# Bucket attention and a rational feed-forward on one core: a table of steps with pair 2's bits, pair 3's k and seven loads in other places

## The chip, the core and the metric

The kernel runs on 1 core of one Trainium2 chip. A core has TensorE (PE, with its weight loads PEld), VectorE (DVE), ScalarE (ACT), GpSimd (POOL) and a queue of transfers on SyncE (SP), which issues in its own order; the transfers of all queues share 16 DMA engines. The metric is device microseconds of one execution.

## What is computed

Two stages follow each other. Attention in which a query sees only keys of its own bucket (six sign bits of a projection), over 4 batches of 8 heads, 768 tokens and 64 channels; then a feed-forward whose activation is a quotient of polynomials, over 3072 tokens.

```python
q_bits = (np.einsum('bhsd,dk->bhsk', q, proj) > 0).astype(np.int64)
k_bits = (np.einsum('bhsd,dk->bhsk', k, proj) > 0).astype(np.int64)
mask = q_bucket[:, :, :, None] == k_bucket[:, :, None, :]
scores = scale * np.matmul(q, k.transpose(0, 1, 3, 2))
scores = np.where(mask, scores, -1000000000.0)
scores = scores - np.max(scores, axis=-1, keepdims=True)
attn = np.exp(scores)
attn = attn / (np.sum(attn, axis=-1, keepdims=True) + 1e-09)
return np.matmul(attn, v).astype(np.float32)
...
h = x @ w_in
P = a[0] + a[1] * h + a[2] * h2 + a[3] * h3
Q = 1.0 + np.abs(b[0]) * np.abs(h) + np.abs(b[1]) * h2
g = P / (Q + 1e-06)
return (g @ w_out).astype(np.float32)
```

w_in and w_out arrive as 64-bit floats, q, k and v as 32-bit floats.

## The kernel before

**Pairs and steps.** Two heads make a pair; there are 16 pairs (0 to 15). A pair's scores are made in 12 steps: six key tiles of 128 for the first 384 queries, then six for the second. In each step TensorE makes two products a head into `pss` (a high part with the mask rows, 77 rows, and a cross product of high and low parts, 128 rows), ScalarE takes their exponential into one of nine tiles E, and GpSimd adds E into a sum `acc`. After six steps TensorE multiplies the six E by v (`psv`, 24 products), and once a pair it adds up `acc` over the partitions (`psu`). A "stretch" of a pair, below, is the time in which its 12 steps run.

**What is prepared ahead.** While a pair's scores run, later pairs are prepared. For a pair p: `load` brings q and k (`qkf`, two transfers of 384 KB); `high` rounds them to the fast matrix format (ScalarE); `low` subtracts, which leaves the low part `lo` (one instruction for q, t=0, one for k, t=1; on VectorE for later pairs, on GpSimd for early ones); `bits` multiplies two pairs at once by the projection (`psb`) and compares on VectorE (`mb`); `penalties` scales the bits; `maskrows` moves them into the operand tiles (four small transfers); `high_move`, `second_low` and `second_high` are transfers that lay the parts out. `maxstep` makes products `psm`, whose row maxima VectorE reduces into `m`; the maxima are transposed (`shift_turn`, TensorE `pst`, VectorE `mt`) and moved in as one more row (`shift_rows`).

**Weights.** Between the steps 32 tiles of weights are turned from 64-bit floats into a high and a low part: even tiles from w_in, odd ones from w_out, 512 KB each into `wr` (two buffers). Tile i has its transfer first, then two operations on ScalarE (`ws`, `wr`), three on VectorE (`psx`), a cast on ScalarE and a subtraction on VectorE. A pair's stretch has one tile of w_in and one of w_out.

**What sets the order.** Every engine and SP's queue run in the order in which the program is written; nothing reorders. The order comes from a table: `at(p, s, f, ...)` (line 501) files a call under the number 12 p + s, and `spread` (line 504) files the steps of a generator, as those of `weights` (line 451). All calls are then made in the order of these numbers, equal ones in the order of filing. The numbers stand in the dictionaries `MID` (most pairs), `FIRST` (pairs 0 to 2), `FIRST3` (pair 3's low parts) and `LAST`. So `load=4.04` in `MID` issues pair p's load behind step 4 of pair p - 4. The buffers of `qkf` are two: pair 4's load needs pair 2's high and low parts and bits done.

**After the pairs** the feed-forward runs in 96 steps of 24 products; in pair 15's stretch its first tokens are read back from memory (`xl`, `xh`).

Of the kernel before, what the change touches and what calls it, by code (L numbers as in the profile page):

```python
# [25 lines left out]
NPAIR = B * NHP  # L26
# [15 lines left out]
MID = dict(  # L42
    group=6, values=[0.66, 0.05], values_col=[1.5, 1.5], values_out=[2.5, 2.5],
    maxima=[6.54, 7.17, 8.32, 9.1, 10.1, 11.02, 12.25, 13.03, 14.15, 15.17, 16.01, 17.02], sums=17.05, sums_store=18.9,
    high=[-0.975, -0.974], low=[-0.946, 3.3, 3.35], bits=-0.945, penalties=4.02, high_move=1.9, maskrows=4.03, second_low=-2.2,
    second_high=2.69, load_v=10.99, shift_turn=5.67, shift_rows=8.82, load=4.04, recips=[23.5, 35.02, 35.3],
    weights=[[1.44, 5.01, 5.015, 5.06, 5.07, 5.08, 5.09, 5.3], [8.05, 11.005, 11.006, 11.022, 11.023, 11.024, 11.0255, 11.0256, 19.32, 21.22]],
    late_weights=[[1.44, 5.1, 5.11, 5.5, 5.65, 5.66, 11.02, 11.023], [8.05, 11.021, 11.022, 11.022, 11.024, 11.0245, 17.05, 17.665, 19.32, 21.22]],
    defer={5: 11.0252, 10: 17.1, 11: 17.2}, weights_last=[0.5, 0.8, 1.0, 1.2],
)  # L50

FIRST = dict(
    maxima1=[-0.072, -0.05, 5.52, 5.97, 6.42, 6.87, 7.32, 7.77, 8.22, 8.67, 9.12, 9.57], maxima2=9.5, rate2=0.82, high=[3.25, 3.53],
    low=[6.0, 7.45], bits=7.4, penalties=7.45, high_move=4.53, maskrows=8.2, second_low=-24.19, second_high=4.35, load_v=4.78, group=2,
    values=[-1.07, 2.65, 2.32, 2.35, 0.35, 0.61], values_out=3.02, high1=[-3.0, -3.2], low1=[-2.8, -2.95],
    high_move1=-2.7, load2=-2.6, load3=3.8, load4=10.2, penalties1=-24.26, maskrows1=-24.2,
    weights=[[-27.25, 5.45, 5.455, 5.55, 5.56, 7.35, 17.55, 18.3], [8.03, 9.04, 9.23, 9.24, 9.25, 9.26, 9.3, 11.9, 12.5, 46.81]],
    warm0=9, warm1=1, warm=3, warms=[3, 3, 3, 0, 1, 0], maxima00=[-4.3, -2.3, -4.2, -0.9, -1.2, -0.8], shift00=[-1.0, -0.2],
    shift0=[-0.08, -0.075], ahead=3, scores=[[-0.85, -0.4, -0.1], [0.1, 0.3, 0.4]], pen01=[-2.9, -0.35],
    second_high0=[-3.42, -3.4, -3.3, -3.25], load_v0=-3.3, bits1=-0.3, comp1=[-0.28, -0.27],  # L60
    maxima0=[-24.05, -23.8, -23.5, -0.9, -0.7, -0.1], turn1=[8.46, 13.26], rows1=[8.6, 14.35], turn2=8.61, third=6.9,
    third_weights=[1.44, 5.01, 5.015, 5.06, 5.07, 5.08, 5.09, 5.3], steps={3: -1.0, 4: -0.8, 5: -0.6, 6: 5.4, 7: 6.5},
)

FIRST3 = dict(low=[0.05, 3.3, 3.35])

LAST = dict(
    group=6, values=[0.28, 0.44], values_out=0.46, vout14=[3.5, 3.03],
    hi14=17.05, weights15=[5.1, 5.11],
    tokens=[[-15.0, -11.5, -8.6, -4.9], [-7.43, -4.5, -2.83, -1.09], [1.1, 4.2, 5.45, 6.3]], terms=1.0, ffn=[13.61, 16.09, 16.14],  # L70
    sums=16.96, wide=8, share=6, third=0, sums14=14.69, weights14=1.44, sumst14=22.46,
)
TINY = 2.0 ** -80

# [35 lines left out]
def bucket_attention_then_rational_ffn(ctx, tc, qT, kT, v, proj, w_in, w_out, coef, consts, out):  # L110
# [56 lines left out]
    def operands_to_terms():  # L167
# [3 lines left out]

    tail.tile([P, 32], F32, tag="below", name="below")
    last = attention(tc, nc, raw, ps_b, tail, tokens, early, operands_to_terms, ffn, load, QF, KF, v, w_in, w_out, wo_d, ident, cst,
                     ones, prj, wi_hi, wi_lo, x_d, s_d, r_d, coefficients)
    ffn.rest(ctx, last)
# [3 lines left out]
def attention(ctx, tc, nc, raw, ps_b, tail, tokens, early, operands_to_terms, ffn, load, QF, KF, v, w_in, w_out, wo_d, ident, cst, ones, prj,  # L179
# [255 lines left out]
    def recips(bb):  # L435
        n = 2 * NHP * S // P
        s = tail.tile([P, n], F32, tag="rs", name=f"rs{bb}")
        nc.sync.dma_start(s, s_d[bb].rearrange("h (x c) -> (h x) c", c=n))
        yield
        z = bank(f"psr{bb}")[:, 0:n] if bb < B - 1 else tail.tile([P, n], F32, tag="rz", name=f"rz{bb}")  # L440
        nc.vector.tensor_scalar(out=z, in0=s, scalar1=0.0, scalar2=1e-9, op0=ALU.is_gt, op1=ALU.mult)
        nc.vector.scalar_tensor_tensor(out=z, in0=z, scalar=S * TINY, in1=s, op0=ALU.max, op1=ALU.add)
        nc.vector.reciprocal(out=s, in_=z)
        yield
        nc.sync.dma_start(r_d[bb].rearrange("h (x c) -> (h x) c", c=n), s)
        yield
# [54 lines left out]
    def at(p, s, f, *args):  # L501
        plan.setdefault(12 * p + s, []).append((f, args))

    def spread(p, steps, gen):
        for s in steps:
            at(p, s, lambda g: next(g, None), gen)

    for p in range(NPAIR):
        mid = 0 < p < NPAIR - 1
        n = MID["group"] if mid else (FIRST if p == 0 else LAST)["group"]  # L510
        for s in range(12):
            if p > 0 or s >= FIRST["ahead"]:
                at(p, FIRST["steps"].get(s, s) if p == 0 else s, scores, p, s)

            if p > 1:
                at(p - 2, FIRST["maxima2"] + FIRST["rate2"] * s if p == 2 else FIRST["third"] if p == 3 and s == 0 else MID["maxima"][s], maxstep, p, s, None, p == 2 or s not in MID["defer"])
                if p > 2 and s in MID["defer"]:
                    at(p - 2, MID["defer"][s], maxreduce, p, s)
            if s % n == n - 1:
                for i in range(s - n + 1, s + 1):  # L520
                    at(p, s + (MID["values"][s // n] if mid else (FIRST if p == 0 else LAST)["values"][s // n]), values, p, i)
            if s % NT == NT - 1 and mid and p < NPAIR - 2:
                at(p, s + MID["values_col"][s // n], values_col, p, s // NT)
            if s % NT == NT - 1:
                at(p, s + (LAST["vout14"][s // NT] if p == NPAIR - 2 else MID["values_out"][s // n] if mid else (FIRST if p == 0 else LAST)["values_out"]), values_out, p, s // NT)
        for hf in range(2):
            at(p, 6 * hf + 9, values_store, p, hf)
        if p < NPAIR - 1:
            at(p, MID["sums"] if p < NPAIR - 2 else LAST["sums14"], sums, p)
            at(p, MID["sums_store"] if p < NPAIR - 2 else LAST["sumst14"], sums_store, p)  # L530
        if p > 1:
            for t in range(2):
                at(p - 2, (MID if p > 2 else FIRST)["high"][t], high, p, t)
                at(p - 2, (MID if p > 3 else FIRST3)["low"][t + t * p % 2] if p > 2 else FIRST["low"][t], low, p, t, nc.vector if p + t > 3 else nc.gpsimd)
            if p % 2 == 0:
                at(p - 2, (MID if p > 2 else FIRST)["bits"], bits, p)
                at(p - 2, (MID if p > 2 else FIRST)["penalties"], penalties, p)
            at(p - 2, (MID if p > 2 else FIRST)["high_move"], high_move, p)
            at(p - 2, (MID if p > 2 else FIRST)["maskrows"], maskrows, p)
        if p > 0:  # L540
            at(p - 1, (MID if p > 1 else FIRST)["second_low"], second_low, p)
            at(p - 1, (MID if p > 1 else FIRST)["second_high"], second_high, p)
            at(p - 1, (MID if p > 1 else FIRST)["load_v"], load_v, p)
        if p > 1:
            at(p - 1, MID["shift_turn"] if p > 2 else FIRST["turn2"], shift_turn, p)
            at(p - 1, MID["shift_rows"], shift_rows, p)
        if p > 3:
            at(p - 4, MID["load"] if p > 4 else FIRST["load4"], load, p)
        if p % NHP == NHP - 1 and p + 1 < NPAIR:
            spread(p, MID["recips"], recips(p // NHP))  # L550
    for i in range(2 * NFC):
# [322 lines left out]
```

## Time and profile before

| | |
|---|---|
| median of 3 runs | 917.94 us (916.36 to 919.22) |
| the profiled execution's own time | 926.93 us |
| its span, first to last instruction | 925.1 us |
| mean granted TensorE clock | 0.991 |
| TensorE busy | 911.5 us (99%) |
| VectorE busy | 832.0 us (90%) |
| ScalarE busy | 652.3 us (71%) |
| GpSimd busy | 428.4 us (46%) |
| moved by DMA | 111.57 MB |

Busy time counts an engine's own instructions; register work, semaphores and the issuing of transfers are left out. A granted clock of 1.00 is TensorE at its higher level of 2.4 GHz, 0.50 at its lower one of 1.2 GHz. All recorded operations carry one source line, L99, a helper's, so the rows below tell them apart by the names of their tiles, in which buffer numbers are left out: `lo<-qkf,k` is a low part of some pair's k.

### The profile page before, as it was taken

To read this page: it belongs to the slowest core of one execution; us is meant where nothing else is said; L and a number is where in the kernel's file an instruction comes from. 1 tells how busy PE (TensorE), PEld (TensorE's weight loads), DVE (VectorE), ACT (ScalarE), POOL (GpSimd) and SP (SyncE) were. 2 spreads that over 40 slices of the span, in tenths; PEclk is the share of its full clock that TensorE was granted. 3 is DMA by queue.
4 is the path that set the end of the run, shared out by engine and by line. 5 is a ranking of instruction groups with operands and counts; after the bars stand their busy time and mean duration, and the time that the engine had idled before them with its cause. 6 is when DMAs were issued, how large, how long until landed. Compare 5 with 4: busy or idle time off the path is not lost.

```text
span 925.1 us, 13694 instructions
## 1 busy us (share of the span) xinstructions
PE 911.5 (99%) x4543; PEld 698.8 (76%) x4543; DVE 832.0 (90%) x1041; ACT 652.3 (71%) x1227; POOL 428.4 (46%) x410
## 2 busy tenths in 40 slices
PE   9979999999999999999999999999999999999998
PEld 5557776776777776678888888888888888888886
DVE  6896888888889887989998999999999999998997
ACT  7446777777777776887777667766676677667664
POOL 7666888787888888012222222222223222222221
PEclk9987999999999999999999999999999999999999
DMA  7685788878888877555402100400040003001001
GB/s 207 173 237 143 221 231 235 234 222 235 230 234 231 230 197 228 162 194 179 150 1 88 49 1 1 137 1 0 1 138 1 1 34 103 1 1 46 1 0 46
DMA packets 51243, 111.57 MB, mean 121 GB/s; under 512 B 9346, under 2 KB 20214, under 8 KB 51172
## 3 DMA queue, kind: packets, MB, share of 16 engines
q1 hardware_dynamic: 50740, 110.47, 40.4%
q8 instruction: 36, 0.59, 0.3%
q14 instruction: 35, 0.29, 0.1%
q10 hardware_dynamic: 432, 0.23, 0.1%
HBM read 56.82 MB, written 21.17 MB: 84 GB/s over the span
## 4 chain that ended last, share of the span: by engine, by line
PE 93%; DMA 3%; DVE 2%; SPq 1%; issue 0%; ACT 0%; DVEq 0%; ACTq 0%
PE psh L99 28%; PE pso L99 28%; PE pss L99 14%; PE psv L99 12%; PE psm L99 7%; DMA wr<-w_in 3%; SPq L99 1%; PE psu L99 1%; PE psb L99 1%; DVE m L99 1%; PE psw L99 1%; DVE psx L99 0%; DMA k<-k 0%; PE pst_None L99 0%; PE pst L99 0%
## 5 line engine op out<-in xcount | busy, mean ns | idle before, releaser
L99 POOL TENSOR_TENSOR gl<-c,gh 128x512 fp32r<-128x512 f32 x95 | 134.9, 1420 | 411.6 <-ACT gh L99 409.5
L99 PE MATMUL pso<-wo,gh 128*128 128x512 f32 x768 | 236.0, 389 | 0.0
L99 POOL TENSOR_TENSOR acc<-acc,E 128x384 f32<-128x384 f32 x232 | 218.6, 978 | 7.4 <-ACT E L99 7.3
L99 ACT ACTIVATE E<-pss 128x384 f32<-128x384 f32 x384 | 168.8, 494 | 73.2 <-PE pss L99 64.8
L99 DVE TENSOR_REDUCE m<-psm 128x1 f32<-128x768 f32 x192 | 180.7, 954 | 28.8 <-PE psm L99 19.5
L99 PE MATMUL pss<-q,k 128*128 128x384 f32 (+2 forms) x768 | 174.0, 350 | 0.1
L99 PEld LDWEIGHTS pso<-wo,gh 128*128 128x128 f32 x768 | 144.2, 188 | 30.0
L99 PE MATMUL psh<-xh,wi_hi 128*128 128x512 f32 x384 | 149.6, 390 | 0.0
L99 ACT ACTIVATE h<-psh 128x512 f32<-128x512 f32 x96 | 57.4, 598 | 130.7 <-PE psh L99 130.7
L99 PE MATMUL psh<-xh,wi_lo 128*128 128x512 f32 x384 | 149.4, 389 | 0.0
L99 PE MATMUL psh<-xl,wi_hi 128*128 128x512 f32 x384 | 149.4, 389 | 0.0
L99 PE MATMUL pso<-wo,gl 128*128 128x512 f32 x384 | 148.9, 389 | 0.0
L99 PEld LDWEIGHTS pss<-q,k 128*128 128x128 f32 (+2 forms) x768 | 136.7, 193 | 15.5 <-issue 8.4
L99 DVE SCALAR_TENSOR_TENSOR c<-c,ab,r 128x512 f32<-128x512 f32 x96 | 136.7, 1424 | 0.0
L99 PE MATMUL psv<-E,v 128*64 128x385 f32 x768 | 133.8, 497 | 0.0
L99 PE MATMUL psm<-k,q 76*128 76x384 f32 (+1 forms) x384 | 102.7, 350 | 6.8 <-DVE m L99 6.0
L99 PEld LDWEIGHTS psv<-E,v 128*64 128x64 f32 x768 | 52.6, 138 | 71.9 <-issue 64.4
L99 DVE SCALAR_TENSOR_TENSOR w<-h,absb,w 128x512 f32<-128x512 f32 x96 | 76.1, 793 | 15.9 <-ACT w L99 15.7
L99 POOL TENSOR_TENSOR acc<-E,E 128x384 f32<-128x384 f32 x58 | 58.4, 1026 | 57.5 <-ACT E L99 57.5
L99 PEld LDWEIGHTS psh<-xh,wi_hi 128*128 128x128 f32 x384 | 72.0, 188 | 16.1 <-ACT r L99 0.6
L99 PEld LDWEIGHTS psh<-xl,wi_hi 128*128 128x128 f32 x384 | 72.1, 188 | 15.0
L99 PEld LDWEIGHTS psh<-xh,wi_lo 128*128 128x128 f32 x384 | 72.1, 188 | 14.9
(89 smaller groups left out, 1188.9 us busy)
## 6 DMA issues: line engine op xcount, KB each, us to landing
q<-q SPq DMA_DIRECT2D x45, 192.0 KB
k<-k SPq DMA_DIRECT2D x45, 192.0 KB
wr<-w_in SPq DMA_DIRECT2D x16, 512.0 KB
wr<-w_out SPq DMA_DIRECT2D x16, 512.0 KB
wo_d<-wr SPq DMA_DIRECT2D x16, 512.0 KB
wo<-wo_d SPq DMA_DIRECT2D x16, 512.0 KB
qkf<-qT SPq DMA_DIRECT2D x16, 384.0 KB
qkf<-kT SPq DMA_DIRECT2D x16, 384.0 KB
```

What stands on the lines that cost most here:

```text
L99: return self.tc.keep_in_program_order(issue(*args, **kwargs))
```

## The change

All but two edits are numbers of the table. Even pairs' loads from pair 6 on are filed at step 11.5 of the pair four ahead, behind v (10.99), where it was 4.04; odd pairs' loads stay at 4.04. In pair 0's stretch pair 2's k low part moves from 7.45 to 6.05 and its bits from 7.4 to 7.31, which is ahead of the values of step 5 (7.32); w_out's first tile is issued at 7.34, pair 4's load at 7.35 (before: 10.2) and the second tile of w_in at 8.8 (before: 13.44). Pair 3's k low part moves from VectorE at 3.3 + 12 to GpSimd at 0.051 + 12. Late in the run a tile of w_in (number 28) and the load of the last v come sooner.

```diff
@@ MID @@
-    second_high=2.69, load_v=10.99, shift_turn=5.67, shift_rows=8.82, load=4.04, recips=[23.5, 35.02, 35.3],
+    second_high=2.69, load_v=10.99, shift_turn=5.67, shift_rows=8.82, load=[11.5, 4.04], recips=[23.5, 35.02, 35.3],
@@ FIRST @@
-    low=[6.0, 7.45], bits=7.4, penalties=7.45, high_move=4.53, maskrows=8.2, second_low=-24.19, second_high=4.35, load_v=4.78, group=2,
+    low=[6.0, 6.05], bits=7.31, penalties=7.315, high_move=4.53, maskrows=8.2, second_low=-24.19, second_high=4.35, load_v=4.78, group=2,
...
-    high_move1=-2.7, load2=-2.6, load3=3.8, load4=10.2, penalties1=-24.26, maskrows1=-24.2,
-    weights=[[-27.25, 5.45, 5.455, 5.55, 5.56, 7.35, 17.55, 18.3], [8.03, 9.04, 9.23, 9.24, 9.25, 9.26, 9.3, 11.9, 12.5, 46.81]],
+    high_move1=-2.7, load2=-2.6, load3=3.8, load4=7.35, penalties1=-24.26, maskrows1=-24.2,
+    weights=[[-27.25, 5.45, 5.455, 5.55, 5.56, 7.317, 17.55, 18.3], [7.34, 9.04, 9.23, 9.24, 9.25, 9.26, 9.3, 11.9, 12.5, 46.81]],
...
-    third_weights=[1.44, 5.01, 5.015, 5.06, 5.07, 5.08, 5.09, 5.3], steps={3: -1.0, 4: -0.8, 5: -0.6, 6: 5.4, 7: 6.5},
+    third_weights=[-3.2, 5.01, 5.015, 5.06, 5.07, 5.08, 5.09, 5.3], steps={3: -1.0, 4: -0.8, 5: -0.6, 6: 5.4, 7: 6.5},
...
-FIRST3 = dict(low=[0.05, 3.3, 3.35])
+FIRST3 = dict(low=[0.05, 3.3, 0.051])
@@ LAST @@
-    sums=16.96, wide=8, share=6, third=0, sums14=14.69, weights14=1.44, sumst14=22.46,
+    sums=16.96, wide=8, share=6, third=0, sums14=14.69, weights14=-1.0, load_v=1.5, sumst14=22.46,
@@ the calls @@
-                at(p - 2, (MID if p > 3 else FIRST3)["low"][t + t * p % 2] if p > 2 else FIRST["low"][t], low, p, t, nc.vector if p + t > 3 else nc.gpsimd)
+                at(p - 2, (MID if p > 3 else FIRST3)["low"][t + t * p % 2] if p > 2 else FIRST["low"][t], low, p, t, nc.vector if p > 3 else nc.gpsimd)
...
-            at(p - 1, (MID if p > 1 else FIRST)["load_v"], load_v, p)
+            at(p - 1, (LAST if p == NPAIR - 1 else MID if p > 1 else FIRST)["load_v"], load_v, p)
...
-            at(p - 4, MID["load"] if p > 4 else FIRST["load4"], load, p)
+            at(p - 4, MID["load"][p % 2] if p > 4 else FIRST["load4"], load, p)
```

GpSimd's queue about the start of pair 1's stretch, before (a name's first number is the pair or tile; the number at its end counts tiles and means nothing here):

```order
L99 TENSOR_TENSOR acc0_1_0_470<-acc0_1_0_470,E2_149 128x384 x2
L99 TENSOR_TENSOR lo0_3_638<-qkf3_421,q1_3_612 128x768
L99 TENSOR_TENSOR acc1_0_0_653<-E3_150,E4_151 128x384 x2
L99 TENSOR_TENSOR acc1_0_0_653<-acc1_0_0_653,E5_152 128x384 x2
L99 TENSOR_TENSOR acc1_0_0_653<-acc1_0_0_653,E6_153 128x384 x2
```

The same place now:

```order
L99 TENSOR_TENSOR acc0_1_0_472<-acc0_1_0_472,E2_149 128x384 x2
L99 TENSOR_TENSOR lo0_3_641<-qkf3_421,q1_3_615 128x768
L99 TENSOR_TENSOR lo1_3_643<-qkf3_421,k1_3_617 128x768
L99 TENSOR_TENSOR acc1_0_0_658<-E3_150,E4_151 128x384 x2
L99 TENSOR_TENSOR acc1_0_0_658<-acc1_0_0_658,E5_152 128x384 x2
L99 TENSOR_TENSOR acc1_0_0_658<-acc1_0_0_658,E6_153 128x384 x2
```

The low part of pair 3's k, lo1_3, stands behind that of its q; it has left VectorE's queue, where it stood between the maxima of steps 7 and 8 of pair 2.

SP's queue from pair 0's to pair 1's stretch, before:

```order
L99 DMA wr1_518<-w_out 128x1024
L99 DMA q1_2_417<-mb2_486 12x768
L99 DMA k1_2_419<-mb2_486 13x768
L99 DMA q1_2_417<-mb2_486 12x768
L99 DMA k1_2_419<-mb2_486 13x768
L99 DMA q1_1_246<-mt1_0_531 1x3x128 x2
L99 DMA x_d0_86<-xo0_0_516 128x384
L99 DMA q2_2_579<-lo0_2_456 64x768 x2
L99 DMA k2_2_580<-lo1_2_497 64x768 x2
L99 DMA qkf4_595<-qT 128x768
L99 DMA qkf4_595<-kT 128x768
...
L99 DMA wr2_660<-w_in 128x1024
```

The same place now:

```order
L99 DMA wr1_500<-w_out 128x1024
L99 DMA qkf4_503<-qT 128x768
L99 DMA qkf4_503<-kT 128x768
L99 DMA q1_2_417<-mb2_479 12x768
L99 DMA k1_2_419<-mb2_479 13x768
L99 DMA q1_2_417<-mb2_479 12x768
L99 DMA k1_2_419<-mb2_479 13x768
L99 DMA q1_1_246<-mt1_0_534 1x3x128 x2
L99 DMA wr2_542<-w_in 128x1024
L99 DMA x_d0_86<-xo0_0_522 128x384
L99 DMA q2_2_585<-lo0_2_456 64x768 x2
L99 DMA k2_2_586<-lo1_2_458 64x768 x2
```

Pair 4's load now stands ahead of pair 2's mask rows, and weight tile 2 ahead of pair 0's output x_d0.

SP's queue at the start of pair 3's stretch, before:

```order
L99 DMA q2_4_1136<-lo0_4_916 64x768 x2
L99 DMA k2_4_1137<-lo1_4_998 64x768 x2
L99 DMA v_3_1156<-v 128x768
L99 DMA wr6_1228<-w_in 128x1024
L99 DMA q1_5_1177<-q1_5_1177 64x768
L99 DMA k1_5_1182<-k1_5_1182 64x768
```

The same place now:

```order
L99 DMA q2_4_1133<-lo0_4_916 64x768 x2
L99 DMA k2_4_1134<-lo1_4_998 64x768 x2
L99 DMA v_3_1153<-v 128x768
L99 DMA qkf6_1196<-qT 128x768
L99 DMA qkf6_1196<-kT 128x768
L99 DMA wr6_1228<-w_in 128x1024
L99 DMA q1_5_1174<-q1_5_1174 64x768
L99 DMA k1_5_1179<-k1_5_1179 64x768
```

Pair 6's load, which stood behind pair 4's mask rows earlier in pair 2's stretch, now stands between pair 3's v and weight tile 6.

## Rows read from the trace of the kernel before

**Rows 1.** The page: busy time of each engine, and two lines of the span in 40 equal slices (busy tenths of TensorE, tenths of its granted clock).

```profile
PE 911.5 (99%) x4543; PEld 698.8 (76%) x4543; DVE 832.0 (90%) x1041; ACT 652.3 (71%) x1227; POOL 428.4 (46%) x410
PE   9979999999999999999999999999999999999998
PEclk9987999999999999999999999999999999999999
```

**Rows 2.** Three stretches of 10 us: their length, then busy us of each engine, the granted clock, the share of the DMA engines and GB/s.

```profile
60.00:70.00 10.00, 4.53 (x17) 4.21 (x18) 8.02 (x10) 2.89 (x8) 1.91 (x3) 0.74 0.56 176
70.00:80.00 10.00, 10.00 (x34) 8.15 (x34) 5.98 (x9) 6.36 (x14) 8.72 (x10) 0.50 0.21 60
80.00:90.00 10.00, 10.00 (x62) 6.36 (x59) 6.40 (x9) 5.18 (x12) 2.37 (x3) 0.91 0.95 235
```

**Rows 3.** TensorE's time line, the row sums of pairs 0 to 3: start us, us, engine, line, operation, out<-in, shape, count.

```profile
54.60 0.85 PE L99 MATMUL psu<-acc,ones 128*32 128x384 f32 x8
...
91.85 0.85 PE L99 MATMUL psu<-acc,ones 128*32 128x384 f32 x8
...
113.99 0.85 PE L99 MATMUL psu<-acc,ones 128*32 128x384 f32 x8
...
137.42 0.85 PE L99 MATMUL psu<-acc,ones 128*32 128x384 f32 x8
```

**Rows 4.** TensorE's time line in pair 1's stretch; in brackets the idle time before a row and what ended it.

```profile
55.38 4.10 PE L99 MATMUL psv<-E,v 128*64 128x385 f32 x24
61.84 0.62 PE L99 MATMUL psm<-k,q 76*128 76x384 f32 x2 [2.35 <-DVE m L99]
...
63.00 0.51 PE L99 MATMUL psm<-k,q 76*128 76x384 f32 x2
67.14 1.01 PE L99 MATMUL psm<-k,q 76*128 76x384 f32 x2 [3.63 <-DVE m L99]
```

**Rows 5.** VectorE's time line in pair 1's stretch and at its end.

```profile
53.20 7.72 DVE L99 TENSOR_TENSOR lo<-qkf,k 128x768 fp32r<-128x768 f32 x1
60.84 1.81 DVE L99 TENSOR_REDUCE m<-psm 128x1 f32<-128x768 f32 x2
...
81.41 0.95 DVE L99 TENSOR_TENSOR lo<-qkf,q 128x768 fp32r<-128x768 f32 x1
```

**Rows 6.** GpSimd's time line in pair 1's stretch.

```profile
49.16 1.85 POOL L99 TENSOR_TENSOR lo<-qkf,q 128x768 fp32r<-128x768 f32 x1 [0.77 <-DMA q<-lo]
50.97 1.99 POOL L99 TENSOR_TENSOR acc<-E,E 128x384 f32<-128x384 f32 x2
52.91 7.19 POOL L99 TENSOR_TENSOR acc<-acc,E 128x384 f32<-128x384 f32 x8
66.09 1.26 POOL L99 TENSOR_TENSOR wi_lo<-ws,wi_hi 128x512 fp32r<-128x512 f32 x1 [6.00 <-ACT wi_hi L99]
```

**Rows 7.** The tile lo over the whole span: engine, operation, count, duration in ns (least, median, most), first and last start in us.

```profile
L99 DVE TENSOR_TENSOR lo<-qkf,k x13: 1265/1504/7718, 53.2 to 341.5; 128x768 fp32r<-128x768 f32 x13
...
L99 POOL TENSOR_TENSOR lo<-qkf,k x3: 1809/1825/1832, 6.9 to 33.6; 128x768 fp32r<-128x768 f32 x3
```

**Rows 8.** SP's time line: the issue of w_in tiles 2, 6, 14 and 28, and of the small store before the last of these.

```profile
50.13 0.43 SPq L99 DMA_DIRECT2D wr<-w_in  x1
...
106.22 0.46 SPq L99 DMA_DIRECT2D wr<-w_in  x1
...
197.67 0.54 SPq L99 DMA_DIRECT2D wr<-w_in  x1
...
358.93 0.40 SPq L99 DMA_DIRECT2D r_d<-rs  x1
359.37 0.45 SPq L99 DMA_DIRECT2D wr<-w_in  x1
```

**Rows 9.** ScalarE's time line: its first operation on the same four tiles.

```profile
57.82 0.68 ACT L99 ACTIVATE ws<-wr 128x512 f32<-128x512 f32 x1 [2.54 <-DMA wr<-w_in]
...
114.20 0.70 ACT L99 ACTIVATE ws<-wr 128x512 f32<-128x512 f32 x1
...
206.26 0.70 ACT L99 ACTIVATE ws<-wr 128x512 f32<-128x512 f32 x1 [0.51 <-DMA wr<-w_in]
...
367.21 0.69 ACT L99 ACTIVATE ws<-wr 128x512 f32<-128x512 f32 x1 [1.97 <-DMA wr<-w_in]
```

**Rows 10.** TensorE's time line: the transposes of maxima that follow tiles 6, 14 and 28.

```profile
118.80 0.27 PE L99 MATMUL pst_None<-cst,m 128*12 128x128 f32 x1
...
210.44 0.28 PE L99 MATMUL pst_None<-cst,m 128*12 128x128 f32 x1
...
371.39 0.28 PE L99 MATMUL pst<-cst,m 128*12 128x128 f32 x1 [1.57 <-DVE m L99]
```

**Rows 11.** Stretches about pair 3's stretch, columns as in rows 2.

```profile
105.00:106.00 1.00, 1.00 (x10) 0.46 (x8) 0.86 (x2) 0.98 (x2) 1.00 (x2) 1.00 1.00 280
106.00:114.00 8.00, 8.00 (x48) 6.72 (x45) 7.82 (x9) 6.67 (x16) 6.54 (x8) 1.00 0.92 255
...
114.00:137.40 23.40, 23.40 (x146) 16.34 (x145) 20.19 (x25) 16.93 (x38) 18.92 (x21) 1.00 0.82 232
```

**Rows 12.** Waits over the whole span: who waited for whom, us in total, times, longest us.

```profile
ACT ws L99 <- DMA wr<-w_in: 5.0, 3, 2.5
...
DVE psx L99 <- DMA wr<-w_out: 5.0, 7, 1.0
```

## Prediction

> **What bounds the kernel now.** I read the page first, then the stretches of 10 us, then the time lines of TensorE, VectorE and GpSimd where a stretch fell out, and last the transfers that one pair's work hangs on. TensorE is busy for 99% of the span and the other engines for less [rows 1], so time is lost only where TensorE idles or runs slowly. The tenths show one such place: its third slice is at 7 and the granted clock dips in slices 3 and 4. In the stretches of 10 us [rows 2] TensorE worked 4.53 us of 60 to 70, with a clock of 0.74, and the clock was 0.50 from 70 to 80 and 0.91 from 80 to 90.
>
> What that costs in all is read from one product that each pair issues once, the row sums psu [rows 3]. From pair 1's to pair 2's it is 22.14 us (91.85 to 113.99), to pair 3's 23.43 (the stretch has the bits psb of two later pairs as well). From pair 0's to pair 1's, which also holds a psb, it is 37.25. So 37.25 - 23.43 = 13.8 us are lost there. The parts: TensorE waited 2.35 and 3.63 us for VectorE's maxima m [rows 4], 6.0 in all; and while it waited its clock fell to 1.2 GHz. Time at half clock is 2 x (0.26 x 10) + 10 + 2 x (0.09 x 10) = 17.0 us [rows 2], of which 2.3 lie in the idle time before 67.14; the other 14.7 us of work would have taken half, so 7.3 are lost. 6.0 + 7.3 = 13.3, and 0.5 stays unassigned.
>
> Why VectorE was late: one subtraction, the low part of pair 3's k, held it for 7.72 us from 53.20 to 60.91 [rows 5]. GpSimd ran without a gap from 49.16 to 60.10, a low part and then ten additions [rows 6], and the subtraction ended 0.8 us after the last of them. The thirteen of this kind on VectorE take 1.27 us at the least and 1.50 at the median [rows 7]. So I take it that something GpSimd held kept this one out. Behind it stood two maxima [rows 5] and VectorE's operations on the weight tile wr2, which ScalarE waited for until 57.82 [rows 9].
>
> **The change, part by part.** (1) Pair 3's low part goes to GpSimd, where one takes 1.83 us [rows 7], and leaves VectorE's queue. With it goes what held the maxima: VectorE is free from 53.3, and the 2.35 and 3.63 us with the clock loss behind them go. What is late next: GpSimd's first ten additions for pair 1 end 1.83 later, at 62 instead of 60.1; a weight subtraction of 1.26 and ten more additions (9.1 for ten) [rows 6] follow, to about 72.4. They are wanted by pair 1's psu, 23.43 us behind 54.60, at 78. Nothing waits. (2) The tile wr2 and pair 4's load are issued ahead of pair 0's first output and leave the crowd in which wr2 took 7.69 us from issue at 50.13 [rows 8] to use at 57.82 [rows 9]. Without that, ScalarE's 2.54 us of waiting and VectorE's operations on wr2 would have been next in line. With (1) and (2) I take the whole 13.8; bounds: 6.0 (if the clock falls anyhow) and 13.8.
> (3) Pair 2's bits ahead of step 5's values, k's low part ahead of one addition: the same products and operations in another order; the only new thing is that pair 4's load (two issues, 768 KB) stands before the four small mask rows of pair 2 on SP's queue. 768 KB (786 thousand bytes) at the 280 GB/s of a microsecond with all engines busy [rows 11] are 2.8 us; the bits come sooner too, and the rows are wanted only by pair 2's maxima, some products later. Bounds 0 to +1.0, taken as 0.
> (4) Even pairs' loads from pair 6 on move from step 4 to behind v, which is ahead of the w_in tile of the next pair's stretch. This happens five times, for pairs 6, 8, 10, 12 and 14, and lands in the stretches of pairs 3, 5, 7, 9 and 11. Queued behind the two new issues are: the w_in tile, the moves of the high parts, second_high, the output store, the mask rows. How near is the tile to being late already? Those that were waited for came 7.69 us after their issue (50.13 to 57.82), 8.59 (197.67 to 206.26) and 7.84 (359.37 to 367.21); the one of pair 3's stretch was used 7.98 after its issue (106.22 to 114.20), without a wait [rows 8, 9]. So it has next to no margin. 768 KB more ahead of it are 2.8 us at a full rate; the 16 engines were at 0.92 over those 8 us [rows 11], so 0.6 of it fills gaps: it lands 2.2 us later. Who waits: VectorE's four operations on the tile stand before the last two maxima of pair 4, and TensorE's transpose pst needs these. Where the tile decided, pst came 4.18 us after ScalarE's first use of it (206.26 to 210.44; 367.21 to 371.39); in pair 3's stretch that would be 114.20 + 4.18 = 118.38, and pst came at 118.80, so 0.4 us of cover [rows 9, 10]. TensorE then idles 2.2 - 0.4 = 1.8 us per stretch. I take 1.6, since of the 16 w_in tiles only those three were waited for [rows 12] and the margin of the other four here can't be seen: 5 x 1.6 = 8.0. Bounds: 0 (the margin is larger than it looks) and 5 x (2.8 - 0.4) = 12.
> What that move gives: the w_out tiles of the even stretches come sooner, and VectorE waited for w_out tiles 7 times, 5.0 us [rows 12]. But TensorE was busy all the time from 114.0 to 137.4 [rows 11], where one of these waits lies, so I count 0; the other end is -1.0.
> (5) The tile wr28 goes ahead of a small store that took 0.40 us to issue [rows 8]. TensorE idled 1.57 us before the pst that depends on it, at 371.39 [rows 10], so -0.3 (0 to -0.4). The last v comes earlier and costs nothing: what it passes is wanted later than it lands.
>
> Sum: -13.8 + 0 + 8.0 - 0.3 = -6.1 us on the profiled execution, 926.93 to 920.8. The median of the runs shown is 917.94, 9.0 less than the profiled one; I take the same difference there: **911.8 us**. Against time 0.3%, some 2.8 us, is what a measurement of this kernel can tell from none.
>
> One rule speaks to part (1). The row: a subtraction on VectorE beside GpSimd's additions took 1.50 us as a rule and 7.72 once [rows 7]. The Trainium skill, "SBUF — State Buffer", section "Who interferes with whom", says that a VectorE instruction with two inputs in SBUF contends with a GpSimd instruction that reads SBUF, and that the one issued first holds the pair of ports for the whole instruction while the other is blocked. By that rule a wait ends with the one addition under way, which the 1.50 fits; the 7.72 is seven additions long, which the rule does not give. By the rule alone the stall would be chance and could come back at pair 4's subtraction.
>
> **Rivals.** A: all is kept. The w_in tiles have margin enough, part (4) costs nothing: 917.94 - 13.8 - 0.3 = 903.8. For it: four of five tiles are not waited for. Against: 7.98 us from issue to use against 7.69 to 8.59 in the waited ones.
> B: the stall moves or was half there. GpSimd's chain runs on to 72.4 and now meets VectorE's next subtraction, for pair 4, which moves from 81.41 [rows 5] to about 67.6; if this is locked out as the other was, TensorE idles some 6.0 us again: -13.8 + 6.0 + 8.0 - 0.3 = -0.1, or 917.8. Or the timed runs, 9.0 us under the profiled one, don't have the clock loss: then -6.0 - 0.3 + 8.0 = +1.7, or 919.6. For it: the 9.0. Against: of the 13 only one was locked out, and the three runs shown lie within 2.9 us, less than a fall of the clock costs.
> C, the slower one: the new waits for the w_in tiles let the clock fall too. If TensorE's 1.6 to 2.4 us of idling per stretch bring it to 1.2 GHz, each fall costs about what the one fall cost, 7.3 us. One fall makes 919.1, two make 926.4. It decides from the second fall on. For it: the clock fell 1.3 us into the second idle time (17.0 us of half clock end at 81.8, so it began at 64.8, and the idle time began at 63.5) [rows 2, 4], after a first wait of 2.35. Against: the 1.57 us at 371.39 [rows 10] left the tenths of the clock at 9 [rows 1]. The Trainium skill, "TensorE: Matmul & The Clock Gate", section "HAM oscillation — how this bites in real kernels", describes such repeated falls behind waits for transfers; whether this case's waits are long enough no row here shows.
>
> **How the numbers follow.** My forecast, stall gone and a part given back, 0.47; A 0.19; B 0.16; C 0.18. The range: its low end is A's with the ends of parts (4) and (5), 903; the high end takes the forecast with 12 us given back and 1.0 from part (3), 917, B's 920, and C with one fall, to 921. Faster by over 0.3% is below 915.2: 0.44 of my forecast, all of A, 0.04 of B, 0.67. Within 0.3%: 0.03 of my forecast, 0.08 of B, 0.02 of C, 0.13. Slower: 0.04 of B, 0.16 of C, 0.20.
>
> **What would show it.** Part (1): psu of pair 0 to psu of pair 1 is 23.4 to 24 us, the clock is 1.00 between, and pair 3's low part is a GpSimd row of 1.8 us. Part (4): ScalarE's first operation on a w_in tile waits for its transfer in the stretches of pairs 3, 5, 7, 9 and 11, and TensorE idles 1 to 2 us before pst there; from psu of pair 2 to psu of pair 3 more than 23.43. Wrong if these stretches stay at 23.4 (then A), if a VectorE subtraction of several us stands at another pair (B), or if the clock shows 0.50 anywhere behind 90 us (C).

## The result, and the profile after

| | before | after |
|---|---|---|
| median of 16 runs each | 919.13 us | 931.35 us |
| fastest and slowest of them | 915.72 to 925.21 | 921.09 to 941.15 |
| ratio after / before | | 1.0109, 95% interval 1.0078 to 1.014 |
| the profiled execution's own time | 926.93 us | 921.10 us |
| its mean granted clock | 0.991 | 1.000 |

The changed kernel is slower; 911.8 us, faster, was predicted. The ratio leaves out runs far above a kernel's fastest, here three of the changed kernel (935 to 941 us, clocks of 0.977 to 0.985), so it stands nearer to 1 than the ratio of the medians.

The two lines on the profiled executions say the opposite of the medians. The one of before is slower than all 16 timed runs of before, the one of after is as fast as the fastest of after. The mean granted clock that is listed with every timed run of after sorts them: 921.09 us at 1.000, 926.65 at 0.996, 930.61 at 0.989, 939.6 at 0.982. Time less (1 - clock) x span, an estimate of what a run would take without half-clock time, is 921.3 us at the median; so some 10 us of the median are clock, and 921.3 is the work and its waits.

The page of after: busy time of each engine, then the tenths of TensorE and of its granted clock; they answer to [rows 1].

```profile
PE 906.0 (99%) x4543; PEld 693.3 (75%) x4543; DVE 825.3 (90%) x1040; ACT 651.8 (71%) x1227; POOL 431.7 (47%) x411
...
PE   8999999999999999999999999999999999999998
...
PEclk9999999999999999999999999999999999999999
```

TensorE's time line of after, the row sums of pairs 0 to 3, beside [rows 3]:

```profile
54.40 0.85 PE L99 MATMUL psu<-acc,ones 128*32 128x384 f32 x8
...
79.38 0.85 PE L99 MATMUL psu<-acc,ones 128*32 128x384 f32 x8
...
101.52 0.85 PE L99 MATMUL psu<-acc,ones 128*32 128x384 f32 x8
...
126.45 0.85 PE L99 MATMUL psu<-acc,ones 128*32 128x384 f32 x8
```

Pair 0's to pair 1's is 24.98 us, where it was 37.25; pair 2's to pair 3's is 24.93, where it was 23.43. The same reading for all five stretches into which a load moved gives +1.50, +1.85, +1.78, +1.40 and +1.57, 8.1 us in all (each the difference of two such intervals). TensorE's time line shows where it stands, once in each of these stretches:

```profile
107.40 0.28 PE L99 MATMUL pst_None<-cst,m 128*12 128x128 f32 x1 [0.99 <-DVE m L99]
...
155.25 0.28 PE L99 MATMUL pst_None<-cst,m 128*12 128x128 f32 x1 [1.53 <-DVE m L99]
...
202.28 0.28 PE L99 MATMUL pst_None<-cst,m 128*12 128x128 f32 x1 [1.12 <-DVE m L99]
...
250.13 0.28 PE L99 MATMUL pst_None<-cst,m 128*12 128x128 f32 x1 [1.03 <-DVE m L99]
...
296.55 0.27 PE L99 MATMUL pst_None<-cst,m 128*12 128x128 f32 x1 [0.46 <-DVE m L99]
```

They are 5.1 of the 8.1 us; a wait for mask rows behind the last, 0.6, is not shown, and the remaining 2.4 the profile does not list as idle time. Behind each is the chain that part (4) named. SP's time line of after at the start of pair 3's stretch, and ScalarE's first operation on that tile (an issue, then the use):

```profile
93.77 0.55 SPq L99 DMA_DIRECT2D qkf<-qT  x1
94.37 0.47 SPq L99 DMA_DIRECT2D qkf<-kT  x1
94.88 0.46 SPq L99 DMA_DIRECT2D wr<-w_in  x1
```

```profile
103.22 0.70 ACT L99 ACTIVATE ws<-wr 128x512 f32<-128x512 f32 x1 [1.36 <-DMA wr<-w_in]
```

The tile takes 8.34 us from issue to use. Counted from psu of pair 2 it is issued at -6.64 us (94.88 - 101.52) and used at +1.70; in before it was issued at -7.77 and used at +0.21 [rows 3, 8, 9]. So of the 1.5 us by which it is used later, 1.1 are the issuing of the load's two transfers ahead of it on SP, and only 0.4 are a longer way of its own. Over the five stretches it is issued 5.5 us later in all and used 7.0 us later. In this execution none of these waits was followed by a fall of the clock; in 14 of the 16 timed runs, by their clocks below 1.000, falls came.

### The profile page after: what moved, and what is told of

Its sections match the earlier page's. It is cut to its first block, busy times and chain, and to the rows that moved or that the text cites. A ratio compares the mean times of both kernels' runs of the same rounds, so it can differ in the third digit from the quotient of the medians.

```text
span 919.3 us, 13688 instructions
## 1 busy us (share of the span) xinstructions
PE 906.0 (99%) x4543; PEld 693.3 (75%) x4543; DVE 825.3 (90%) x1040; ACT 651.8 (71%) x1227; POOL 431.7 (47%) x411
## 4 chain that ended last, share of the span: by engine, by line
PE 93%; DMA 4%; DVE 2%; SPq 1%; issue 0%; ACT 0%; POOL 0%; DVEq 0%; ACTq 0%; POOLq 0%
PE psh L99 28%; PE pso L99 28%; PE pss L99 14%; PE psv L99 12%; PE psm L99 7%; PE psu L99 1%; PE psb L99 1%; DVE m L99 1%; DMA k<-k 1%; DMA wr<-w_in 1%; SPq L99 1%; DMA x_d<-xo 1%; DMA q<-mb 1%; DMA v<-v 0%; DMA qkf<-qT 0%
## 5 line engine op out<-in xcount | busy, mean ns | idle before, releaser
L99 PE MATMUL pss<-q,k 128*128 128x384 f32 (+2 forms) x768 | 171.9, 346 | 0.1
L99 PEld LDWEIGHTS pss<-q,k 128*128 128x128 f32 (+2 forms) x768 | 133.8, 189 | 16.8 <-issue 8.8
L99 DVE SCALAR_TENSOR_TENSOR c<-c,ab,r 128x512 f32<-128x512 f32 x96 | 138.7, 1445 | 0.0
L99 PE MATMUL psv<-E,v 128*64 128x385 f32 x768 | 131.9, 492 | 0.0
L99 PE MATMUL psm<-k,q 76*128 76x384 f32 (+1 forms) x384 | 100.7, 345 | 2.7 <-DVE m L99 1.0
L99 DVE SCALAR_TENSOR_TENSOR w<-h,absb,w 128x512 f32<-128x512 f32 x96 | 72.8, 759 | 15.9 <-ACT w L99 15.7
L99 PEld LDWEIGHTS pso<-wo,gl 128*128 128x128 f32 x384 | 72.1, 188 | 15.0
```

The lines of the kernel that those rows point to most:

```text
L99: return self.tc.keep_in_program_order(issue(*args, **kwargs))
```

## The experiments

Each kernel ran beside the kernel before on the same chip. All medians first, then each with what was expected. The clock is the median over a kernel's timed runs.

| | median, us (runs) | clock | ratio to before, 95% |
|---|---|---|---|
| 1 before again | 920.75 (10) | 0.9935 | 1.0024 (0.9992 to 1.0055) |
| 2 after, loads back | 914.03 (10) | 0.999 | 0.9943 (0.9921 to 0.9965) |
| 3 before, loads moved | 939.27 (4) | 0.985 | 1.0177 (1.0106 to 1.0248) |
| 4 before, pair 3's k low moved | 918.96 (10) | 0.996 | 0.9987 (0.9961 to 1.0014) |
| 5 after, w_in tiles first | 932.95 (4) | 0.988 | 1.0148 (1.0123 to 1.0172) |
| 6 before, first stretch's edits | 914.68 (10) | 0.9985 | 0.9976 (0.9938 to 1.0013) |
| 7 after, 8 products a wait | 926.28 (6) | 0.995 | 1.0087 (1.0047 to 1.0127) |
| 8 after, loads behind tiles | 940.3 (4) | 0.981 | 1.0265 (1.0202 to 1.0328) |
| 9 before, one tile sooner | 915.78 (10) | 0.999 | 0.9962 (0.994 to 0.9983) |
| 10 after, 18 products a wait | 930.39 (4) | 0.999 | 1.012 (1.009 to 1.015) |
| 11 as 6, more rounds | 914.97 (10) | 0.998 | 0.9945 (0.9928 to 0.9962) |
| 12 as 2, more rounds | 914.16 (6) | 0.9995 | 0.9933 (0.9907 to 0.9959) |

**Experiment 1: before, unchanged.**

> The kernel before, unchanged, so that the granted clock of each of its timed runs is listed. Theory 1 (waits in front of a late w_in tile let TensorE's clock fall in the timed runs of the changed kernel; the kernel before rarely has such a fall): most runs here have a clock of 0.998 or more and take 915 to 920 us; a run with a clock near 0.991 takes 925 or more. Theory 2 (the timed runs of before have the fall as the profile has, and the 9 us between them are something else): clocks near 0.991 throughout. The profile taken again shows whether the 37.25 us from psu of pair 0 to psu of pair 1 are a constant of this kernel or chance: with the stall and the fall 37, with the stall alone 29 to 30, without either 23.5 to 24.5.

Neither theory held as it was put: the clocks of the ten runs lie anywhere from 0.990 to 0.998, none at 1.00, and the time follows them (915.8 at 0.997, 926.95 at 0.991). Without half-clock time the estimate is 914.9 us. So before has a fall in nearly every run, of differing length. The profile shows that the fall doesn't need the stall that the prediction saw. VectorE's time line: the subtraction that was held for 7.72 us [rows 5] took 1.52 here; TensorE's: it waits all the same, once, for the mask rows.

```profile
52.71 1.52 DVE L99 TENSOR_TENSOR lo<-qkf,k 128x768 fp32r<-128x768 f32 x1
```

```profile
63.29 0.73 PE L99 MATMUL psm<-k,q 76*128 76x384 f32 x2 [2.40 <-DMA k<-mb]
```

Why the mask rows are late is on SP's time line of the same profile (starts and lengths of issues), with ScalarE's first use of the tile wr2 under it:

```profile
49.61 1.32 SPq L99 DMA_DIRECT2D wr<-w_in  x1
51.03 0.82 SPq L99 DMA_DIRECT2D q<-q  x1
51.95 0.57 SPq L99 DMA_DIRECT2D k<-k  x1
52.61 1.60 SPq L99 DMA_DIRECT2D q<-mt  x2
54.26 1.16 SPq L99 DMA_DIRECT2D q<-q  x2
55.49 3.09 SPq L99 DMA_DIRECT2D k<-k  x2
58.85 0.36 SPq L99 DMA_DIRECT2D x_d<-xo  x1
59.92 0.84 SPq L99 DMA_DIRECT2D q<-mb  x1
```

```profile
58.18 0.70 ACT L99 ACTIVATE ws<-wr 128x512 f32<-128x512 f32 x1 [3.38 <-DMA wr<-w_in]
```

From 49.61 SP issues eight transfers, wr2 the oldest; the ninth, the second of the last k<-k, stands in its row until 58.11 and goes out as wr2 has landed (ScalarE takes it at 58.18). It waits by order of the program: in the trace SP's transfers use eight completion semaphores in turn, and each waits for the transfer that used the same one before it, here wr2, which was complete at 58.10. SP's own waits from 54 to 64 us list it (who, us in total, times, longest):

```profile
SPq L99 <- DMA wr<-w_in: 2.0, 1, 2.0
```

The mask rows q<-mb and k<-mb, issued from 59.92 on, stand behind that. After TensorE's 2.40 us the clock is low, as the stretches of 10 us from 60 on show (columns as in [rows 2]):

```profile
60.00:70.00 10.00, 7.60 (x28) 7.12 (x27) 6.00 (x8) 5.44 (x13) 5.92 (x7) 0.68 0.56 177
70.00:80.00 10.00, 10.00 (x44) 5.79 (x47) 6.23 (x8) 5.12 (x9) 4.92 (x6) 0.64 0.59 162
```

**Experiment 2: after, with the loads put back.**

```diff
- load=[11.5, 4.04]
+ load=[4.04, 4.04]
```

> The changed kernel with even pairs' loads back at step 4.04 (part 4 undone, all else kept). Theory 1: from psu to psu the stretches of pairs 3, 5, 7, 9 and 11 are 23.4 us again where they were 24.8 to 25.7, the profile takes 921.1 - 8.1 = 913, and since the waits that let the clock fall are gone the timed runs lie at 911 to 916 with clocks of 0.998 or more. Rival (the falls come from the other parts, GpSimd's added low part or the earlier tile and load in pair 0's stretch): the stretches shorten, yet the timed runs keep clocks of 0.985 to 0.993 and lie at 920 to 928.

914.03 us, 913.4 to 916.1, clocks of 0.998 to 1.000: theory 1 as expected, rival out. The row sums of pairs 0 to 3:

```profile
55.18 0.85 PE L99 MATMUL psu<-acc,ones 128*32 128x384 f32 x8
...
80.15 0.85 PE L99 MATMUL psu<-acc,ones 128*32 128x384 f32 x8
...
102.26 0.85 PE L99 MATMUL psu<-acc,ones 128*32 128x384 f32 x8
...
125.83 0.85 PE L99 MATMUL psu<-acc,ones 128*32 128x384 f32 x8
```

Pair 2's to pair 3's is 23.57 again. All that the change costs lies in part (4): 931.35 - 914.03 = 17.3 us. Of these 8.1 are the stretches, by the profiles; the rest goes with the clocks, at the median 0.989 and 0.999.

**Experiment 3: before, with the loads moved and nothing else.**

```diff
- load=4.04
+ load=[11.5, 4.04]
```

> The kernel before with part 4 alone: even pairs' loads at step 11.5. Theory 1: odd stretches of 24.8 to 25.7 us, 8 us more, and falls of the clock on top: timed runs at 928 to 940, 10 to 20 over before, with clocks of 0.980 to 0.993. Rival (part 4 costs only its 8 us of waiting, the falls come from elsewhere): 925 to 928 with clocks as before's.

928 to 968 us with clocks from 0.996 down to 0.957: theory 1, though one run, 967.99 at 0.957, lies far beyond its 940 and its 0.980 as well; the rival's 925 to 928 is passed by all four runs. TensorE's waits in pair 1's and pair 3's stretches:

```profile
64.56 0.59 PE L99 MATMUL psm<-k,q 76*128 76x384 f32 x2 [2.30 <-DMA k<-mb]
113.14 0.28 PE L99 MATMUL pst_None<-cst,m 128*12 128x128 f32 x1 [1.83 <-DVE m L99]
```

**Experiment 4: before, with pair 3's k low part on GpSimd.**

```diff
- FIRST3 = dict(low=[0.05, 3.3, 3.35])
+ FIRST3 = dict(low=[0.05, 3.3, 0.051])
- nc.vector if p + t > 3 else nc.gpsimd
+ nc.vector if p > 3 else nc.gpsimd
```

> The kernel before with part 1 alone: pair 3's k low part on GpSimd behind that of its q. The first stretch, psu of pair 0 to psu of pair 1, falls from 37 us to 24 or 25 in the profile. If the timed runs of before have the two waits of 6.0 us without the fall of the clock, this takes 5 to 6 us: 912 to 914. If they have the fall too: 905. If the lock-out of VectorE's subtraction is chance and mostly absent from the timed runs: 917 to 919, no difference.

918.96 us, no difference: part (1) alone brings nothing. The first stretch is 28.15 us in the profile, not 24 or 25. The wait for the mask rows is there and the clock falls behind it, if for less long than in experiment 1:

```profile
63.25 0.59 PE L99 MATMUL psm<-k,q 76*128 76x384 f32 x2 [2.13 <-DMA k<-mb]
```

```profile
60.00:70.00 10.00, 7.87 (x37) 7.37 (x36) 7.18 (x10) 6.20 (x15) 8.27 (x10) 0.83 0.60 188
70.00:80.00 10.00, 10.00 (x66) 6.26 (x65) 8.32 (x11) 7.03 (x15) 5.45 (x7) 1.00 0.83 220
```

**Experiment 5: after, with w_in tiles 4 to 26 ahead of the loads.**

```diff
- weights=[[1.44, 5.01, ...
+ weights=[[-1.0, 5.01, ...
```

> The changed kernel with the w_in tiles 4 to 26 issued ahead of the even pairs' loads (at -1.0 instead of 1.44), the loads left at 11.5. Theory 1 (what costs the 8.1 us and the falls is that the tile stands behind 768 KB on the queue): odd stretches 23.4 to 23.8 us, 913 to 915, clocks of 0.998 or more, as with the loads put back. Rival (the late load itself, or the crowd of transfers in that stretch whatever their order): odd stretches stay at 24.5 or more and the time above 919.

The rival: 932.95 us, no better. The tile no longer is what is waited for, and the mask rows, further back on the same queue, are late instead. The profiled execution is the slowest of the four, 948.66 us. The waits of the whole profile (who, us in total, times, longest), the first of them in pair 3's stretch on TensorE's time line, and the granted clock there:

```profile
PE psm L99 <- DMA q<-mb: 7.4, 4, 2.5
```

```profile
111.18 0.72 PE L99 MATMUL psm<-k,q 76*128 76x384 f32 x2 [1.85 <-DMA q<-mb]
```

```profile
110.00:120.00 10.00, 8.82 (x28) 8.85 (x29) 4.21 (x5) 4.40 (x9) 6.64 (x8) 0.57 0.65 218
```

So the order of tile and load isn't the cause; that the load stands at the start of that stretch at all is, as experiment 2 shows. How it delays the rest is shown in part. One way is SP's queue: the load takes two more issues and two of the eight semaphores, and from 95 to 109 us SP's waits list 1.6 us for the tile and 1.6 us for the load before the mask rows go out. The other, which no run here shows by itself, may be the DMA engines' share: 94 to 106 us, first of after, then of experiment 2 (columns as in [rows 2]).

```profile
94.00:98.00 4.00, 4.00 (x25) 3.23 (x20) 4.00 (x5) 2.92 (x8) 2.53 (x4) 1.00 0.98 264
98.00:102.00 4.00, 4.00 (x29) 3.36 (x27) 3.71 (x4) 3.45 (x9) 4.00 (x5) 1.00 1.01 292
102.00:106.00 4.00, 4.00 (x32) 1.63 (x24) 2.47 (x4) 1.97 (x4) 4.00 (x5) 1.00 1.02 236
```

```profile
94.00:98.00 4.00, 4.00 (x25) 2.86 (x22) 4.00 (x5) 2.79 (x7) 2.58 (x3) 1.00 0.84 226
98.00:102.00 4.00, 4.00 (x25) 3.94 (x23) 3.84 (x5) 3.58 (x9) 3.98 (x5) 1.00 1.00 240
102.00:106.00 4.00, 4.00 (x28) 1.51 (x29) 3.50 (x6) 2.82 (x6) 4.00 (x4) 1.00 0.84 228
```

With the load there the engines are full for 12 us; without it they have (0.16 + 0.16) x 4 = 1.3 us left. Windows that start 0.74 us later, as far behind psu as those of after, leave 2.0. So by an estimate 0.8 to 1.5 of the 2.8 us that the prediction gave the load (from [rows 11]) don't fit in; the stretch of after grew by 1.5, and the two issues on SP alone move its tile by 1.1.

**Experiment 6: before, with the edits to pair 0's stretch alone** (pair 2's bits and k low, pair 4's load, tiles 1 and 2).

```diff
- low=[6.0, 7.45], bits=7.4, penalties=7.45 ... load4=10.2
+ low=[6.0, 6.05], bits=7.31, penalties=7.315 ... load4=7.35
- weights=[[..., 5.56, 7.35, ...], [8.03, ...]], third_weights=[1.44, ...
+ weights=[[..., 5.56, 7.317, ...], [7.34, ...]], third_weights=[-3.2, ...
```

> The kernel before with the edits to pair 0's stretch alone (pair 2's bits and k's low part, pair 4's load, weight tiles 1 and 2 sooner); pair 3's k low part stays on VectorE, the loads at 4.04. Theory 2 (not the subtraction but the wait of 2.1 to 2.4 us for pair 2's mask rows, which the profiles of the first two experiments on before's table show, is what let the clock fall in before, and the sooner tile and bits remove it): first stretch 24.5 to 25.5 us without an idle TensorE of over 1 us, clocks of 0.998 or more, time 913 to 915. Rival (the prediction's part 1: the subtraction on VectorE is the cause): the wait stays, 917 to 920, as the experiment with the subtraction alone had gained nothing only because something else was late next.

Theory 2: 914.68 us, the first stretch 24.97 us in the profile, with the subtraction still on VectorE. Two of the ten runs took 925 and 927, for which the expectation has no place; with them the ratio isn't clear of 1. Experiment 11 takes them up.

**Experiment 7: after, with eight products before pst_None in five stretches.**

```diff
+ if p % 2 == 0 and 2 < p < NPAIR - 2:
+     for _ in range(8):
+         nc.tensor.matmul(ps[:, P:512], K1[p - 1][0:77, 0, 0:P], Q1[p - 1][0:77, 0, 0:HQ], start=True, stop=True)
  nc.tensor.transpose(ps[0:n, 0:P], m, ident)
```

> The changed kernel with eight more products (77 x 128 by 384, about 1.4 us at full clock, their output unused) put on TensorE just before the transposes pst_None of pairs 4, 6, 8, 10 and 12, where it waits 1.5 us each. Theory 1 (these waits are what lets the clock fall): the stretches stay at about 25 us, the waits in the profile shrink under 0.5 us, the clocks of the timed runs rise from a mean of 0.990 to 0.997 or more and the time falls from 931 to 921 to 925. Rival (the falls come from elsewhere): clocks stay near 0.990 and the time at 931 or above (up to 7 us more for the added products).

Half of it came: clocks of 0.992 to 1.000, 922.4 to 932 us, a median of 926.28 beside 931.35 although there is more work; the median clock of 0.995 misses 0.997. The profile caught the other half: four of the five waits were gone, at the fifth the tile was so late that TensorE still idled, and there alone the clock fell.

```profile
251.95 0.28 PE L99 MATMUL pst_None<-cst,m 128*12 128x128 f32 x1 [1.92 <-DVE m L99]
```

```profile
250.00:260.00 10.00, 8.08 (x29) 7.76 (x29) 6.12 (x9) 5.03 (x11) 4.94 (x6) 0.66 0.70 232
```

**Experiment 8: after, with the loads behind the w_in tiles.**

```diff
- load=[11.5, 4.04]
+ load=[13.5, 4.04]
```

> The changed kernel with even pairs' loads still later, at 13.5, which is behind the w_in tile of the next stretch (1.44). Theory 1: the tile is in front again and lands in time; odd stretches back to 23.4 to 24, 913 to 916, clocks of 0.998 or more, unless the load itself then comes too late for its pair's high parts. Rival (the load's place in the odd stretch costs in any order): 919 or more.

The rival again, as in experiment 5: 940.3 us, and TensorE waits for mask rows. Of its five such waits, 1.08, 0.73, 2.24, 1.67 and 1.77 us, the clock fell behind the longest alone:

```profile
204.06 0.59 PE L99 MATMUL psm<-k,q 76*128 76x384 f32 x2 [2.24 <-DMA q<-mb]
```

```profile
204.00:214.00 10.00, 9.94 (x34) 9.53 (x34) 5.39 (x6) 5.41 (x12) 7.97 (x9) 0.54 0.63 209
```

**Experiment 9: before, with the second w_in tile sooner and nothing else.**

```diff
- third_weights=[1.44, ...
+ third_weights=[-3.2, ...
```

> The kernel before with one number changed: the second w_in tile (wr2) issued at 8.8 instead of 13.44; bits, pair 4's load and pair 3's low part as before. Theory 2, now in full: in before ScalarE waits for wr2 (until 58), behind it in its queue stands pair 0's output, behind that on SP's queue pair 3's mask rows, and TensorE's psm waits 2.1 to 2.4 us for these. Then this one number brings all of it: first stretch 24.5 to 25.5 us, no wait for k<-mb, 913.5 to 916, clocks of 0.998 or more. Rival (the sooner bits or load of pair 2 and 4 are needed as well): the wait stays at 1 us or more and the time at 916 to 920.

One number brings most of it: 915.78 us, five of ten runs at a clock of 1.000. The wait for the mask rows is not all gone, and the stretch is 25.70 us:

```profile
62.00 0.58 PE L99 MATMUL psm<-k,q 76*128 76x384 f32 x2 [0.74 <-DMA k<-mb]
```

So the tile is the cause of most of it. The other edits to this stretch may be worth the last microsecond (914.03 to 914.97 in experiments 2, 6, 11 and 12), about the 0.74 us of waiting left here, but the intervals overlap. The chain in the expectation is wrong in one link: SP itself stood, as experiment 1 shows, not ScalarE's output in front of it.

**Experiment 10: as 7, with eighteen products.**

```diff
- for _ in range(8):
+ for _ in range(18):
```

> As the experiment with eight products before pst_None, with eighteen (3.15 us at full clock). The wait there is 1.5 us in the changed kernel, so about 1.6 us of the products a stretch are added to the path, 8 us in all: 921.3 + 8 = 929 if the clock holds. Theory 1 (the waits let the clock fall): clocks of 0.998 or more in nearly all runs and 928 to 931, with a spread under 4 us, although more work is done than in the changed kernel. Rival (falls from elsewhere): clocks near 0.990 and 936 to 941.

Theory 1: 929.8 to 932.6 us, of which one run of four lies above the 931, a spread of 2.8 us and clocks of 0.998 to 1.000. TensorE's time line in pair 3's stretch, and the page's clock:

```profile
107.08 3.39 PE L99 MATMUL pst_None<-q,k 77*128 77x384 f32 x18
110.31 0.27 PE L99 MATMUL pst_None<-cst,m 128*12 128x128 f32 x1
```

```profile
PEclk9999999999999999999999999999999999999999
```

The tile is as late as before; only the idle time is filled. That takes the falls away and so shows that they came with these waits. It is no cure: the products cost what they save.

**Experiments 11 and 12: as 6 and as 2, in more rounds.**

> The edits to pair 0's stretch alone, again, with more rounds, beside the next one: two of ten runs had taken 925 and 927, as the kernel before did in the profile where VectorE's subtraction for pair 3 was held for 7.72 us. Theory 3 (that hold is chance, and pair 3's low part on VectorE leaves it possible): one to four of the 16 runs at 922 to 928, the others at 913.5 to 917.

> The changed kernel with the even pairs' loads back at 4.04, again, with more rounds: pair 3's low part is on GpSimd here. Theory 3: no run above 918, median 914. Rival (the two slow runs of the other kernel had nothing to do with that subtraction): one to four of 16 above 920 here too. It is also the version that should beat both kernels: a ratio to before of 0.993 to 0.996.

Theory 3 found no support: no run of experiment 11 is above 916.7 us, of ten where the expectation counted on 16, and the two of experiment 6 have no explanation here. The six runs of experiment 12 lie at 912.0 to 915.2, as expected. In the profiles of the five experiments that keep this subtraction on VectorE and have it beside GpSimd's additions (1, 3, 6, 9, 11) it took 1.06 us in experiment 9 and 1.50 to 1.56 in the other four. The changed kernel with its loads put back beats both kernels: 0.9933 (0.9907 to 0.9959) of before, and 17 us under the change as made.

## Why the prediction was wrong

**Part (4), right in size.** 5 x 1.6 = 8.0 us were forecast, 8.1 measured, at the place named: a w_in tile waited for, VectorE late with m, TensorE idle before pst_None. The reason given was too narrow. It made the tile, standing behind the load's bytes, the one that is late. In after most of that lateness is the time that SP takes to issue the load, 1.1 of 1.5 us in pair 3's stretch, so that the size was met in part by luck; and experiments 5 and 8 put the tile in front and the mask rows were late instead (in experiment 8 the four stretches without a fall grew by 1.0 to 2.0 us).

**Parts (1) and (2), the wrong one credited.** The prediction read the first stretch's loss from one execution and put it down to the subtraction held for 7.72 us. That hold is real in [rows 5], but it came once in six profiles in which it could. What the other profiles of a table with before's first stretch show (experiments 1, 3 and 4) is in part (2): wr2, late in the crowd, holds SP's queue and with it the mask rows, and TensorE waits 2.1 to 2.4 us for these. The prediction had wr2 only as "next in line". Experiment 4 undoes the credit of part (1), experiment 9 gives it to wr2. The term was mis-sized too: -13.8 takes 23.43 us as this stretch's floor, but at full clock and without an idle moment it has 24.97 us of work (experiment 2: 55.18 to 80.15), so -12.3 was to be had in that execution. In the timed runs it is worth about 5 us (experiment 2 beside before, 914.03 to 919.3).

The rule on the shared ports that was weighed there, from the Trainium skill, "SBUF — State Buffer", section "Who interferes with whom", had it the better way round: by it a subtraction waits for the one addition under way and no longer. The five durations of 1.06 to 1.56 us agree; what held the one of 7.72 past seven additions stays open.

**Part (5), unclear.** The stretch from pair 13's to pair 14's psu is 15.82 us after and was 17.45; but experiment 1, unchanged, has 16.30 and experiment 4, without the edit, 15.80.

**The step that failed: carrying the sum to the median.** "I take the same difference there" assumed that before's profiled execution and its timed runs differ by a constant that the changed kernel has too. The sum itself came out, 920.8 forecast and 921.10 measured, and partly by luck: between the two profiles -13.8, +8.0 and -0.3 measured -12.3, +8.1 and -1.6, and -13.8 held a hold that was chance. But the 9.0 us were that hold and a longer fall of the clock in one execution, not an offset. Set up from the estimates without half-clock time, the change is 914.9 to 921.3, +6.4: a wait of 2 us goes and 8.1 come. The clock adds the rest: some 4 to 6 us of falls a run in before, 10 in after, and +12.2 between the medians. In the prediction's own terms, in the timed runs, -13.8 was worth about -5, and +8.0 cost 17.3 (experiment 2), since the sum had no term for the clock behind the new waits.

**The rivals.** B's second half (the timed runs don't have that clock loss) and C (the new waits let the clock fall) were both true at once, and each had been weighed as if the other were false: B's 919.6 with C's falls on top lies near 930. C was argued down by one wait of 1.57 us that no fall followed [rows 10]. That row was right and said little, for the length of a wait alone doesn't decide. No fall stood behind the 0.46 to 1.53 us of after, the 1.67 and 1.77 of experiment 8, the 1.83 of experiment 3, or the longest of experiment 5 (TensorE's time line there, and the granted clock around it):

```profile
218.28 0.59 PE L99 MATMUL psm<-k,q 76*128 76x384 f32 x2 [2.47 <-DMA q<-mb]
```

```profile
215.00:225.00 10.00, 7.53 (x42) 6.34 (x42) 5.12 (x7) 5.76 (x14) 5.41 (x7) 1.00 0.67 206
```

One followed 1.81 in the same profile and each of those shown above with 1.85, 1.92, 2.13, 2.24, 2.30 and 2.40. And one and the same wait differs from run to run (2.40, 2.30 and 2.13 us in experiments 1, 3 and 4), so that a table with five such places can meet a long one often. The timed runs have no trace, so that it was longer waits that made their falls is inferred; that the falls go when these waits are filled is shown by experiment 10. The Trainium skill, "TensorE: Matmul & The Clock Gate", section "HAM oscillation — how this bites in real kernels", tells of a clock that falls again and again behind waits for transfers; experiment 10, in which the clock holds once the same waits are filled, agrees.

Not tried: odd pairs' loads moved as well, a load split into two halves in the two places, and more than eight semaphores for SP's transfers.

## What to carry to other kernels

A stall with a clock fall behind it has no fixed price: before a profile's loss is booked as a gain, compare the profiled execution's time and clock with those of the timed runs, and look for the part that comes back in a second profile. A transfer that is moved into a stretch costs its queue issuing time there (1.1 us for the two of a load) besides bytes, and here something was late in each of three orders; and waits of a microsecond or two in five places, 8.1 us in all, cost as much again through TensorE's clock. Where a queue issues in order, ask what each issue waits for, and what its oldest unfinished transfer holds up, not only who reads that transfer.

## What was not expected of the hardware

In experiment 1 SP's queue stood for 2.0 us until a transfer landed that it had issued eight places before: nothing goes out until 58.11 us, and wr2 is complete at 58.10. No run here shows a limit of the queue itself in this; it is the semaphore that comes round after eight transfers. So a late 512 KB tile delayed four small moves that had nothing to do with it.

After nearly the same wait the clock's fall differs: behind 2.40 us (experiment 1) the next two stretches of 10 us have 0.68 and 0.64, behind 2.13 (experiment 4) 0.83 and 1.00, that is 6.8 us of lost clock and 1.7 (10 x what is missing to 1.00). That fits the spread of one unchanged kernel over 11 us, with clocks from 0.990 to 0.998 (experiment 1).
